# A test of all softmax row sums on the chip, with a second program behind a branch, and a newly written order of all work

## The chip, the core and the metric

The kernel runs on one core of one Trainium2 chip. A core has five engines, each with its own queue of instructions: TensorE (PE in the profile, its weight loads PEld), VectorE (DVE), ScalarE (ACT), GpSimd (POOL) and SyncE (SP, which here only issues transfers and waits). They meet only through semaphores. The metric is device microseconds of one execution; less is better. The profile is of one execution of the program on the chip, and it has a time of its own.

## The reference

For 2048 tokens `x` of width 512 the kernel computes a mix of two branches, `g * a + (1 - g) * b`, with one gate per token, `g = sigmoid(sum(x * gate_w))`.

Branch `a` is attention with 32 heads of width 16 over 4 segments of 512 tokens each, with a memory that is carried from segment to segment:

```
logits = einsum('bhqd,bhkd->bhqk', qs, ks) * scale + mask
p = softmax(logits, axis=-1)
a_dot = einsum('bhqk,bhkd->bhqd', p, vs)
num = einsum('bhld,bhde->bhle', phi(qs), M);  den = einsum('bhld,bhd->bhl', phi(qs), z) + 1e-6
o = g_head * num / den + (1 - g_head) * a_dot
M = M + einsum('bhld,bhle->bhde', phi(ks), vs);  z = z + sum(phi(ks))
```

`phi(t)` is `t + 1` above zero and `exp(t)` below; the mask is causal within a segment; `a` is `o @ wo`. Branch `b` is a gated feed-forward block: `(gelu(x @ w_gate) * (x @ w_up)) @ w_down`, 512 to 1792 to 512. Everything is given and returned in bf16. The reference's softmax subtracts the largest logit of each row before it takes the exponential.

## The kernel before, in words

The kernel takes the exponential of the scaled logits as they are, without a row maximum. The row sums come out of the same product as the weighted values: the tile of values, `vnat`, has a 17th column of ones for each head, so row 16 of each product is the sum of that row's exponentials. Both are turned by VectorE, the sum is inverted (`rc`, L650) and multiplied in (L651).

The work is cut into small tasks. A task names its engine, the instructions and the keys of what it reads and writes; `Emitter.plan` and `Emitter.finalize` derive from these keys every semaphore wait. In which order the tasks stand in each engine's queue is written out by hand, as one long string `ORDER` (L850 to L930): `Sched.schedule` walks through its words, and each word is a task's name, with the PSUM bank that it takes behind a colon, or `a` or `d` where the task may go to ScalarE or VectorE. No time is computed when the kernel is built; an engine runs its tasks strictly in this order and waits where one is not ready.

For each segment `s` and each tile there are these tasks:

- `K`, `Q`, `V`, `G`, `U`: products of four matmuls of 128x512 into one of four PSUM banks (`dense`, L446), each followed by an eviction `Kev`, `Qev`, `Vev`, `Gev` on ScalarE (L438) or VectorE (L439), or by the GELU (`gd`, `gelu`, ScalarE) or the product with it (`h`, VectorE, L689).
- `st`: a fill, logits of four heads at once into the one score tile `psX` of 128x2048 (L597); `exp`: the exponential of all of it on ScalarE (L603); `msk`: the causal mask of the diagonal blocks on GpSimd (L609). There are 72 fills. As `psX` exists once, a fill waits for the exponential of the fill before it.
- `pv`: 64 small matmuls that multiply the exponentials with the values (L640); `tp`: VectorE turns the two banks (L516); `pvp`: the inverse of the row sums and the scaling (L650, L651); `ot`: adds the memory's part (L657) and turns the result (L659) for `wo`.
- `nz`, `nd`, `mz`, `gate` on TensorE and `ndp`, `nzp`, `mzacc`, `phq`, `phk` on other engines: the memory and the gate.
- `out` (L702) and `wo` (L719): the two output products; `wev` scales the first on ScalarE (L707) or VectorE (L710), `oev` on VectorE adds the second (L723), and `dma` stores 128 rows of the output (L728), the last row tile in two halves, one issued by SP and one by ScalarE.

Weights and `x` are loaded in the first third (L329, L333). TensorE begins with some matmuls on constants (`wake`, L368), then turns the first part of `x` (`xtr0`, L774). At the end SP waits for each of the 17 output stores (L827), and the closing of the block (L806) gathers all engines.

The last words of `ORDER` before:

```
... pv3_3:31 tp3_d31:0 out3_2_2 tp3_d30:1 out3_1_4 out3_2_3
out3_2_4 wev3_1:a dma11_0 pvp3_31 out3_3_0:1 pvp3_30 ot3_3 out3_3_1 wo3_0_0:0 oev3_0_0 dma12_0 wo3_1_0:3 out3_3_2
out3_3_3 out3_3_4 oev3_1_0 wo3_2_1:0 wo3_2_0:3 wev3_2:a wo3_3_0:2 oev3_2_1 oev3_2_0 wo3_3_1:0 wev3_3:a dma13_0
oev3_3_0 dma14_1 dma15_0 oev3_3_1 dma15_1
```

Of the kernel before, what the change touches and what calls it, by code (L numbers as in the profile page):

```python
# [16 lines left out]
H = 32  # L17
# [6 lines left out]
ZMAX = 60.0  # L24
R_PT = 6
# [115 lines left out]


class Emitter:
# [75 lines left out]
    def emit(self, eng):  # L219
        e = self.engmap[eng]  # L220
        for spec in self.streams[eng]:
            for sem, val in spec.waits:
                e.wait_ge(sem, val)
            ins = spec.fn(e)
            if spec.dma_sem is not None:
                ins.then_inc(spec.dma_sem, 16)
            elif spec.inc:
                ins.then_inc(self.cnt[eng], 1)
# [7 lines left out]
def _build(es, nc, A_x, A_wq, A_wk, A_wv, A_wo, A_beta, B_w_gate, B_w_up, B_w_down, gate_w, out):  # L236
# [45 lines left out]
    rc = [sb(f"rc{i}", [P, 16], F32) for i in range(R_TT)]  # L282
# [14 lines left out]
    S = Sched({"bank": N_BANK, "X": 1, "tT": R_TT})  # L297
    I = Instr

    def task(name, ways, lat):  # L300
        return S.add(Task(name, ways, lat))

    def one(name, eng, est, instrs, lat=None):
        if lat is None:
            lat = {PE: L_PE, ACT: L_ACT, DVE: L_DVE, POOL: L_POOL, SP: 0.0}[eng]
        return S.add(Task(name, [(eng, est, instrs)], lat))

    def bk(s):
        return ("bank", s)


    def load(name, eng, fn, writes, issue=0.52, lat=2.5, size=0.0, wait=()):
        t = one("ld_" + name, eng, issue, [I(fn, wait, [*writes, ("ld", name)], sem("s_" + name))],
                lat=lat)
        t.size = size

    wgr = B_w_gate.rearrange("(kb p) n -> p kb n", p=P)
    wur = B_w_up.rearrange("(kb p) n -> p kb n", p=P)
    wdr = B_w_down.rearrange("(fb p) n -> p fb n", p=P)
    wsrc = lambda a: a.rearrange("(kb p) n -> p kb n", p=P)  # L320
    halves = (slice(0, 2), slice(2, 4))
    ball = omem[:, 1, 0:H]
    stage = (R_PT - 1,)

    def x_of(i, kb):
        return [("xT", i, kb, q) for q in range(4)]

    def ld_w(name, eng, dst, src, writes, size, wait=()):
        load(name, eng, lambda e: e.dma_start(dst, src), writes, size=size, wait=[("ld", w) for w in wait])  # L329

    def ld_xt(s, behind="wo30"):
        for kb in range(4):
            load(f"x{s}_{kb}", SP, lambda e, kb=kb: e.dma_start_transpose(  # L333
                xT[s % R_XT][:, kb, :], A_x[0, s * 512:(s + 1) * 512, kb * 128:(kb + 1) * 128]),
                x_of(s % R_XT, kb), issue=1.31, size=0.28, wait=[("ld", behind)])

    for q, (eng, n) in enumerate(((SP, 1), (ACT, 1), (SP, 2))):
        ld_w(f"x0_{q}", eng, pt[stage[0]][:, q:q + n, :],
             A_x[0, 128 * q:128 * (q + n), :].rearrange("(q p) d -> p q d", p=P), [("xs", q + j) for j in range(n)],
             0.125 * n)  # L340
    for h, eng in enumerate((ACT, SP)):
        ld_w(f"wk{h}", eng, wk[:, halves[h], :], wsrc(A_wk)[:, halves[h], :], [("wk", 2 * h), ("wk", 2 * h + 1)], 0.25)
    for h in range(2):
        ld_w(f"wq{h}", SP, wq[:, halves[h], :], wsrc(A_wq)[:, halves[h], :], [("wq", h)], 0.25)
    load("gw", SP, lambda e: e.dma_start(gatew[:, :], gate_w.rearrange("(kb p) -> p kb", p=P),
                                         allow_slow_non_contiguous=True), [("gatew",)], wait=[("ld", "x0_2")])
    ld_w("wv", SP, wv[:], wsrc(A_wv), [("wv",)], 0.5, ["x0_2"])
    ld_w("beta", SP, ball, A_beta.partition_broadcast(P), [("ball",)], 0.02, ["wk0"])
    ld_xt(1, "wv")
    ld_w("wg0", SP, wg[:, halves[0], :], wgr[:, halves[0], :], [("wg", 0)], 0.9, ["wq0"])  # L350
    ld_w("wg1", SP, wg[:, halves[1], :], wgr[:, halves[1], :], [("wg", 1)], 0.9, ["wv"])
    ld_w("wu0", SP, wu[:, halves[0], :], wur[:, halves[0], :], [("wu", 0)], 0.9, ["x1_3"])
    ld_w("wu1", SP, wu[:, halves[1], :], wur[:, halves[1], :], [("wu", 1)], 0.9, ["wg0"])
    ld_w("wd0", SP, wd[:, 0:HFT, :], wdr[:, 0:HFT, :], [("wd", 0)], 0.9, ["wg1"])
    ld_w("wd1", SP, wd[:, HFT:NFT, :], wdr[:, HFT:NFT, :], [("wd", 1)], 0.9, ["wu0"])

    wo32 = A_wo.rearrange("(x i) n -> x i n", i=32)
    for t in range(4):
        for i, (c0, c1, x) in enumerate(((0, t + 1, t), (t + 1, 4, 4 * (t + 1) + 3))):
            if c0 < c1:  # L360
                ld_w(f"wo{t}{i}", SP, wo[32 * c0:32 * c1, t, :], wo32[x:x + 3 * (c1 - c0 - 1) + 1:3], [("wo", t, i)],
                     0.03125 * (c1 - c0), ["wu1"])
    ld_xt(2)


    s0 = Slot("X")
    for i, cols in enumerate(([512] * 5 + [128] * 3, [128] * 1)):
        one(f"wake{i}", PE, 3.2, [I(lambda e, c=c: e.matmul(  # L368
            XALL[:, 0:c], nc.const_aps.tensor(1.0, [P, P], BF), nc.const_aps.tensor(1.0, [P, c], BF),
            start=True, stop=True), [], [("X", s0)]) for c in cols])  # L370
    cn = [
        I(lambda e: e.memset(maskA[:], 0.0), writes=[("maskA",)]),
    ]
    for g in range(4):
        cn.append(I(lambda e, g=g: e.memset(maskA[32 * g:32 * g + 16, :], 1.0), [("maskA",)], [("maskA",)]))
    cn.append(I(lambda e: e.tensor_scalar(maskB[:], maskA[:], -1.0, 1.0, ALU.mult, ALU.add),
                [("maskA",)], [("maskB",)]))
    one("masks", POOL, 1.0, cn)
    one("vones0", DVE, 1.22, [I(lambda e: e.memset(vnat[0][:, :, :, :, 16:17], 1.0),
                               writes=[("vnat", 0, m) for m in range(4)])])  # L380

    for i in range(2):
        cc = ctri[i][:, :]
        one(f"causal{i}", POOL, 0.3, [
            I(lambda e, cc=cc: e.memset(cc, 1.0), writes=[("ctri", i)]),
            I(lambda e, cc=cc, i=i: e.affine_select(out=cc, in_=cc, compare_op=ALU.is_ge, fill=0.0, base=64 * i,
                                                    pattern=[[1, 64]], channel_multiplier=-1),
              [("ctri", i)], [("ctri", i)])])
    causal = ctri[1]
    one("causal", DVE, 0.1, [I(lambda e: e.tensor_copy(causal[0:64, :], ctri[0][0:64, :]), [("ctri", 0), ("ctri", 1)],  # L390
                               [("causal",)])])
    one("ident", POOL, 0.6, [
        I(lambda e: e.memset(ident[:], 0.0), writes=[("ident",)]),
        I(lambda e: e.affine_select(out=ident[:], in_=ident[:], compare_op=ALU.not_equal, fill=1.0, base=0,
                                    pattern=[[-1, 128]], channel_multiplier=1), [("ident",)], [("ident",)]),
    ])
    cn = [
        I(lambda e: e.memset(bdmask[:], 1.0), writes=[("bdmask",)]),
    ]
    cn.append(I(lambda e: e.affine_select(out=bdmask[:], in_=bdmask[:], compare_op=ALU.is_ge, fill=0.0, base=0,  # L400
                                          pattern=[[-16, 8]], channel_multiplier=1), [("bdmask",)], [("bdmask",)]))
    cn.append(I(lambda e: e.affine_select(out=bdmask[:], in_=bdmask[:], compare_op=ALU.is_ge, fill=0.0, base=15,
                                          pattern=[[16, 8]], channel_multiplier=-1), [("bdmask",)], [("bdmask",)]))

    for c in range(4):
        cn.append(I(lambda e, c=c: e.tensor_copy(zmask[:, c, 2 * c:8], bdmask[:, 0:8 - 2 * c]), [("bdmask",)], [("zmask",)]))
        if c:
            cn.append(I(lambda e, c=c: e.tensor_copy(zmask[:, c, 0:2 * c], bdmask[:, 8 - 2 * c:8]), [("bdmask",)], [("zmask",)]))
    cn.append(I(lambda e: e.memset(mzacc[:], 0.0), writes=[("mzacc",)]))
    cn.append(I(lambda e: e.memset(vnat[1][:, :, :, :, 16:17], 1.0), writes=[("vnat", 1, m) for m in range(4)]))  # L410
    one("consts", POOL, 4.2, cn)


    def gate_products(h, sl):
        one(f"gate{h}", PE, 0.5, [I(lambda e, i=i, kb=kb, s=s: e.matmul(  # L415
            BK[sl.i][32 * i:32 * i + 1, 256 + 128 * (s % 2):384 + 128 * (s % 2)], gatew[:, kb:kb + 1],
            xT[s % R_XT][:, kb, :].rearrange("p (q j r) -> p j q r", j=4, r=32)[:, i],
# [88 lines left out]
    def slot_of(t, g):  # L506
        return (t - g) % 4

    def quad(c):
        return slice(32 * c, 32 * c + 32)  # L510
# [448 lines left out]
```

## Time and profile before

| what | value |
|---|---|
| median of 3 runs | 265.19 us (265.04 to 265.82) |
| the profiled execution's own time | 265.16 us |
| its span, first to last instruction | 263.4 us |
| time outside the span | 1.76 us |
| granted TensorE clock | 1.00 of full speed |
| PE busy | 259.6 us of the span |
| DVE, ACT, POOL busy | 200.3, 210.7, 96.4 us |

A page of the profile has numbered parts: 1 is the busy time of each engine, 2 the span in 40 slices of 6.6 us with the busy share in tenths, 3 the transfer queues, 4 the chain of work that ended last, 5 the costliest groups of instructions with what ended the idle time before them, 6 the issued transfers. Beside it the trace answers with the instructions in order of time (a timeline: start, duration, engine, line, operation, output and inputs), with the durations of one line's instructions, with who waited for whom, and with the busy time of each engine in a given stretch. Register, branch, semaphore and transfer-issuing instructions belong to an engine's sequencer (a "q" behind its name) and don't count as busy. The ends of matmuls are modelled, so that their durations overlap; from start to start a 128x512 matmul takes 0.216 us here.

### The profile page before, as it was taken

What the parts mean: (1) busy time and instruction counts of PE and PEld (TensorE: products, weight loads), DVE (VectorE), ACT (ScalarE), POOL (GpSimd) and SP (SyncE); (2) the same over time, 40 slices, a digit from 0 to 9 for tenths busy, and PEclk for the clock granted to TensorE, in tenths of its full rate; (3) what the DMA queues carried; (4) which work ended last, traced back from release to release, by engine and by line L of the source; (5) the groups of instructions that cost most, each with busy time, mean ns of one, the idle gap of its engine ahead of it and who ended that gap; (6) DMA issues with size and microseconds to landing.
All of it is one profiled execution on the core that took longest, in us unless ns stands there. A gap on an engine that the chain in (4) does not pass through costs nothing.

```text
span 263.4 us, 6630 instructions
## 1 busy us (share of the span) xinstructions
PE 259.6 (99%) x2829; PEld 113.4 (43%) x2829; DVE 200.3 (76%) x373; ACT 210.7 (80%) x174; POOL 96.4 (37%) x159
## 2 busy tenths in 40 slices
PE   8999999999999999999999999999999999999996
PEld 4633434444343443544434344444444443444443
DVE  1577767678896775988999998866779786865964
ACT  3589799998888978999888698759989968478612
POOL 6025233055536106144351844423635044152700
PEclk9999999999999999999999999999999999999999
DMA  7996188910045210000005200010002000010002
GB/s 229 281 184 169 37 109 194 257 56 2 0 55 99 70 40 0 2 4 20 2 0 85 59 2 2 20 33 0 2 4 74 2 2 0 2 60 2 20 2 80
DMA packets 24155, 14.92 MB, mean 57 GB/s; under 512 B 14526, under 2 KB 23102, under 8 KB 24126
## 3 DMA queue, kind: packets, MB, share of 16 engines
q1 hardware_dynamic: 23566, 14.04, 24.5%
q8 instruction: 22, 0.36, 0.6%
q10 hardware_dynamic: 560, 0.46, 0.5%
q14 instruction: 7, 0.06, 0.1%
HBM read 8.14 MB, written 2.10 MB: 39 GB/s over the span
## 4 chain that ended last, share of the span: by engine, by line
PE 97%; DMA 1%; DVE 0%; SPq 0%; issue 0%
PE psD L446 53%; PE psD L702 19%; PE psX L597 9%; PE psD L640 7%; PE psD L719 5%; DMA pt<-in_A_x_dram 1%; PE psD L468 1%; PE psD L474 1%; PE psD L565 1%; PE psD L415 0%; PE psX L541 0%; PE psD L531 0%; DVE ost L723 0%; PE psX L774 0%; SPq L329 0%
## 5 line engine op out<-in xcount | busy, mean ns | idle before, releaser
L603 ACT ACTIVATE pt<-psX 128x2048 bf16<-128x2048 f32 x72 | 135.1, 1876 | 31.7 <-PE psX L597 31.0
L609 POOL TENSOR_TENSOR pt<-pt,ctri 128x256 bf16<-128x256 bf16 x128 | 91.2, 720 | 152.0 <-ACT pt L603 147.6
L446 PE MATMUL psD<-xT,wu 128*128 128x512 bf16 x224 | 56.7, 380 | 0.0
L446 PE MATMUL psD<-xT,wg 128*128 128x512 bf16 x224 | 55.0, 380 | 0.0
L702 PE MATMUL psD<-wd,gb 128*128 128x512 bf16 x224 | 54.7, 380 | 0.0
L689 DVE TENSOR_TENSOR gb<-psD,gb 128x512 bf16<-128x512 f32 x56 | 37.3, 683 | 15.0 <-PE psD L446 14.7
L702 PEld LDWEIGHTS psD<-wd,gb 128*128 128x128 bf16 x224 | 20.4, 98 | 25.9 <-issue 3.3
L446 PEld LDWEIGHTS psD<-xT,wu 128*128 128x128 bf16 x224 | 20.2, 98 | 26.1 <-issue 3.4
L446 PEld LDWEIGHTS psD<-xT,wg 128*128 128x128 bf16 x224 | 20.3, 98 | 25.9 <-issue 3.0
L516 DVE STREAM_TRANSPOSE tT<-psD 128x512 f32<-128x512 f32 x35 | 24.1, 703 | 8.5 <-PE psD L640 8.0
L597 PE MATMUL psX<-qT,kD 32*128 32x192 bf16 (+7 forms) x512 | 28.5, 287 | 0.0
L597 PEld LDWEIGHTS psX<-qT,kD 32*128 32x128 bf16 x512 | 8.2, 92 | 24.9 <-ACT pt L603 18.9
L640 PE MATMUL psD<-pt,vnat 64*17 64x128 bf16 (+7 forms) x512 | 18.7, 283 | 0.0
L640 PE MATMUL psD<-pt,vsh 64*17 64x128 bf16 (+7 forms) x512 | 18.3, 283 | 0.0
L651 DVE SCALAR_TENSOR_TENSOR ob<-tT,gq,rc 128x256 bf16<-128x256 f32 x32 | 17.1, 534 | 1.1
L446 PE MATMUL psD<-wv,xT 128*128 128x512 bf16 x64 | 17.3, 380 | 0.0
L723 DVE SCALAR_TENSOR_TENSOR ost<-psD,gtok,wds 128x512 bf16<-128x512 f32 (+1 forms) x18 | 12.2, 686 | 6.2 <-PE psD L719 6.1
L446 PE MATMUL psD<-xT,wq 128*128 128x512 bf16 x64 | 16.6, 380 | 0.0
L719 PE MATMUL psD<-wo,oT 128*128 128x512 bf16 (+1 forms) x72 | 16.2, 356 | 0.0
L640 PEld LDWEIGHTS psD<-pt,vnat 64*17 64x17 bf16 x512 | 11.6, 86 | 8.7 <-POOL pt L609 4.0
L680 ACT ACTIVATE gb<-psD 128x512 bf16<-128x512 f32 x28 | 14.9, 606 | 0.3 <-PE psD L446 0.2
L439 DVE CAST gb<-psD 128x512 bf16<-128x512 f32 x18 | 11.9, 681 | 4.0 <-PE psD L446 4.0
(95 smaller groups left out, 253.9 us busy)
## 6 DMA issues: line engine op xcount, KB each, us to landing
out_dram<-ost SPq DMA_DIRECT2D x15, 128.0 KB, 1.8
wg<-in_B_w_gate_dram SPq DMA_DIRECT2D x2, 896.0 KB, 6.7
wu<-in_B_w_up_dram SPq DMA_DIRECT2D x2, 896.0 KB, 5.7
wd<-in_B_w_down_dram SPq DMA_DIRECT2D x2, 896.0 KB, 7.5
vsh<-vnat SPq DMA_DIRECT2D x16, 68.0 KB, 2.2
wq<-in_A_wq_dram SPq DMA_DIRECT2D x2, 256.0 KB, 5.1
wv<-in_A_wv_dram SPq DMA_DIRECT2D x1, 512.0 KB, 5.2
wk<-in_A_wk_dram ACTq DMA_DIRECT2D x1, 256.0 KB, 3.9
```

The source lines that it names most:

```text
L446: one(f"{name}{'abcd'[h // 2]}", PE, 2 * T_MM, [I(lambda e, i=i: e.matmul(BK[sl.i][:, :], lhs(i), rhs(i), start=(i == 0), stop=(i == n - 1 ...
L516: one(f"tp{name}", DVE, 0.605, [I(lambda e, ts=ts, bank=bank: e.transpose(tT[ts.i][:, :], bank()), [key], [("tT", ts)])])
L597: ins.append(I(lambda e, c=c, kb=kb, ncol=ncol, c0=c0, g=g: e.matmul(XALL[:, g * 512 + c0:g * 512 + c0 + ncol], kD[b][quad(g), c, kb, :], ...
L603: one(f"exp{s}_{name}", ACT, 2048 * 0.000833 + 0.05, [I(lambda e: e.activation(pt[slot][:, :, :], xin, ACTF.Exp, scale=ATT_SCALE), [("X", ...
L609: ins.append(I(lambda e, mv=mv: e.tensor_tensor(mv, mv, cm, ALU.mult), [("pt", slot), ("causal",)], [("pt", slot)]))
L640: ins.append(I(lambda e, kb=kb, slot=slot, c0=c0, n=n, g=g, c=c, r0=r0, sl=banks[j], va=va: e.matmul(BK[sl.i][32 * c:32 * c + 17, 64 * kb: ...
L651: I(lambda e, ts=ts, t=t, j=j, dst=dst: e.scalar_tensor_tensor(out=dst, in0=t_rows(ts, 16), scalar=gq[:, 2 * t + j:2 * t + j + 1], in1=rc_ ...
L680: one(f"gd{s}_{ft}", ACT, 0.485, [I(lambda e, gi=gi, f=f, sl=sl: e.activation(gb[gi][:, f, :], BK[sl.i][:, :], ACTF.Gelu_apprx_tanh), [bk( ...
L689: one(f"h{s}_{ft}", DVE, 0.605, [I(lambda e, sl=sl, gi=gi, f=f: e.tensor_tensor(gb[gi][:, f, :], BK[sl.i][:, :], gb[gi][:, f, :], ALU.mult ...
L702: mm.append(I(lambda e, fb=fb, gi=gi, f=f, q=q, sl=sl: e.matmul(BK[sl.i][:, :], gb[gi][:, f, q], wd[:, fb, :], start=(fb == 0), stop=(fb = ...
L719: one(f"wo{s}_{qt}_{ci}", PE, 4 * T_MM / len(parts), [I(lambda e, kb=kb, q=q, so=so, c=c: e.matmul(BK[so.i][:, c], oT[:, kb, q], wo[:, kb, ...
L723: lambda e, so=so, gt=gt, wi=wi, oi=oi, c=c: e.scalar_tensor_tensor(out=ost[oi][:, c], in0=BK[so.i][:, c], scalar=gtok[:, gt:gt + 1], in1= ...
```

## The change

Three things change.

**The test.** The inverted row sums no longer go to three rotating small tiles, but to `rcall`, one place for each of two segments, four tiles and two halves (128x128 numbers for a segment). After the four attention tiles of a segment, VectorE tests all of them (`chk0` to `chk3`): clamp to 1e-10 and 1e10, compare with the unclamped, take the minimum over the row. At the end `okrow` takes the minimum over the four segments, TensorE sums it over the 128 partitions (`oksum`, one matmul with one column), VectorE copies the sum to SBUF (`flag`), and each of the five engines loads it into a register (`reg_pe` and so on).

**The second program.** The build function is wrapped into `program(exact)` and called twice. Behind the first program each engine compares its register with 128.0 and, where it differs, runs the second program, the whole computation again with row maxima subtracted; where it is equal, it jumps over it. The second program doubles each fill's matmuls, and adds 512 products with two VectorE instructions each, three terms for each maximum, and 96 small transfers in each segment. SP's waits for the 17 stores stand behind the jump.

**The order.** `ORDER` is written anew for all tasks, with the new ones in it. 36 evictions change between ScalarE and VectorE; on balance six move to VectorE.

The core of the diff, without the re-indentation:

```diff
+RC_LO, RC_HI = 1e-10, 1e10
+GOOD = 0x43000000
...
-    rc = [sb(f"rc{i}", [P, 16], F32) for i in range(R_TT)]
+    rcall = sb("rcall", [P, 2, 4, 2, 16], F32)
+    okall = sb("okall", [P, NSEG], F32)
+    okrow = sb("okrow", [P, 1])
+    flag = sb("flag", [1, 1], F32)
...
+    def program(exact):
...
-                        qT[b][quad(g), c, 512 - ncol:512], start=True, stop=True, tile_position=(32 * g, 0)),
+                        qT[b][quad(g), c, 512 - ncol:512], start=True, stop=not exact, tile_position=(32 * g, 0)),
...
+                r, kr = rcall[:, b, t, j, :], ("rc", b, t, j)
                 one(f"pvp{s}_{t}{j}", DVE, 0.70, [
-                I(lambda e, ts=ts: e.reciprocal(rc[ts.i][:, :], tT[ts.i][:, 16:512:32]), [("tT", ts)], [("rc", ts)]),
+                    I(lambda e, ts=ts, r=r: e.reciprocal(r, tT[ts.i][:, 16:512:32]), [("tT", ts)], [kr]),
...
+        def test_rows(s):
+            r = rcall[:, s % 2].rearrange("p t j c -> p (t j c)")
+            kr = [("rc", s % 2, t, j) for t in range(4) for j in range(2)]
+            y = gt[:, 0:128]
+            one(f"chk{s}", DVE, 0.7, [
+                I(lambda e: e.tensor_scalar(y, r, RC_LO, RC_HI, ALU.max, ALU.min), kr, [("gt",)]),
+                I(lambda e: e.tensor_tensor(y, y, r, ALU.is_equal), [*kr, ("gt",)], [("gt",)]),
+                I(lambda e: e.tensor_reduce(okall[:, s:s + 1], y, mybir.AxisListType.X, ALU.min), [("gt",)], [("ok", s)])])
+            if s < NSEG - 1:
+                return
+            one("okrow", DVE, 0.1, [I(lambda e: e.tensor_reduce(okrow[:, :], okall[:, :], mybir.AxisListType.X, ALU.min),
+                                      [("ok", i) for i in range(NSEG)], [("okrow",)])])
+            sl = Slot()
+            one("oksum", PE, 0.1, [I(lambda e: e.matmul(BK[sl.i][:, 0:1], nc.const_aps.tensor(1.0, [P, P], BF), okrow[:, :],
+                                                        start=True, stop=True), [("okrow",)], [bk(sl)])])
+            one("flag", DVE, 0.1, [I(lambda e: e.tensor_copy(flag[:, :], BK[sl.i][0:1, 0:1]), [bk(sl)], [("flag",)])])
+
+            def fetch(e, eng):
+                regs[eng] = e.alloc_register(f"ok_{eng}")
+                return e.reg_load(regs[eng], flag.bitcast(mybir.dt.int32)[0:1, 0:1])
+
+            for eng in ENGINES:
+                one(f"reg_{eng}", eng, 0.1, [I(lambda e, eng=eng: fetch(e, eng), [("flag",)])])
...
+    def run(e, eng):
+        em.emit(eng, parts[0][eng])
+        with e.If_ne(regs[eng], GOOD):
+            em.emit(eng, parts[1][eng])
...
         @block.sync
         def _(e):
-            em.emit(SP)
+            em.emit(SP, parts[0][SP])
+            with e.If_ne(regs[SP], GOOD):
+                em.emit(SP, parts[1][SP])
+                for name in outs:
+                    e.wait_ge(sem(name), 32)
             for name in outs:
                 e.wait_ge(sem(name), 16)
...
 ORDER = """
...
+wev3_1:a tp3_d30:2 tp3_d31:1 out3_2_4 pvp3_30 pvp3_31 out3_3_0:1 out3_3_1 ot3_3 wo3_0_0:0 oev3_0_0 wo3_1_0:3 oev3_1_0
+out3_3_2 dma12_0 out3_3_3 chk3 wev3_2:a out3_3_4 okrow wo3_2_0:0 oev3_2_0 wo3_2_1:3 oev3_2_1 wo3_3_0:2 dma13_0
+wev3_3:a wo3_3_1:0 oev3_3_0 oev3_3_1 dma14_1 dma15_1 oksum:3 flag dma15_0 reg_pe reg_act reg_dve reg_pool reg_sp
```

## The prediction

> **What bounds the kernel now.** I read the page's head and queues first, then the busy time of each engine in three stretches, then the chain of work, and last the end of the run instruction by instruction.
>
> ```profile
> span 263.4 us, 6630 instructions
> PE 259.6 (99%) x2829; PEld 113.4 (43%) x2829; DVE 200.3 (76%) x373; ACT 210.7 (80%) x174; POOL 96.4 (37%) x159
> DVE  1577767678896775988999998866779786865964
> ...
> q8 instruction: 22, 0.36, 0.6%
> ...
> q14 instruction: 7, 0.06, 0.1%
> ...
> PE 97%; DMA 1%; DVE 0%; SPq 0%; issue 0%
> ```
>
> ```profile
> 4.86:260.82 255.96, 255.93 (x2812) 111.48 (x2812) 199.19 (x370) 209.16 (x173) 93.24 (x137) 1.00 0.25 54
> 260.82:263.40 2.58, 0.00 (x0) 0.00 (x0) 0.52 (x2) 0.00 (x0) 0.00 (x0) 1.00 0.33 102
> ```
>
> The columns of the second view are the stretch, its length, and the busy time of PE, PEld, DVE, ACT and POOL, then clock, transfer share and GB/s. TensorE has work in 255.93 of the 255.96 us from 4.86 to 260.82, at full clock. Its modelled ends could hide gaps, so I took the starts too: of 550 pairs of neighbouring 128x512 matmuls at L446 the mean distance is 217 ns and the usual one 216, and the distance before a fill is 316 on average with 309 to 312 as the usual one. Over the whole stretch I find some 0.4 us that a better order could still take out. The time is thus 4.9 us of start, 256 us of TensorE, and a tail of 2.6 us without TensorE, which is the stretch that the change reaches:
>
> ```profile
> 258.91 1.91 PE L719 MATMUL psD<-wo,oT 128*128 128x256 bf16 x16
> 259.11 0.69 ACT L707 ACTIVATE wds<-psD,omgt 128x512 f32<-128x512 f32 x1 [1.07 <-PE psD L702]
> 259.55 1.80 DVE L723 SCALAR_TENSOR_TENSOR ost<-psD,gtok,wds 128x256 bf16<-128x256 f32 x4 [1.41 <-PE psD L719]
> 261.38 0.36 ACTq L728 DMA_DIRECT2D out_dram<-ost  x1
> ```
>
> ```profile
> L806 PEldq DRAIN  x1: 775/775/775, 260.1 to 260.1; - x1
> ...
> L806 SPq COMPARE_BRANCH  x1: 41/41/41, 263.0 to 263.0; - x1
> L806 SPq DRAIN  x1: 13/13/13, 263.2 to 263.2; - x1
> ```
>
> ```profile
> L827 SPq EVENT_SEMAPHORE  x8: 28/28/28, 261.4 to 263.0; - x8
> ```
>
> The last VectorE instruction ends at 261.34, ScalarE issues the last store at 261.38, and it lands 1.6 us later (the page has 1.6 for both half stores). SP's eight waits lie between 261.36 and 262.96; those with nothing to wait for start 0.07 us apart. Then SP branches and drains, and the block closes 0.47 us after the last wait. TensorE is through at 260.87 and waits for the others.
>
> **The change, part by part.** The sum is made against the profiled execution's 265.16 us (span 263.4 and 1.76 around it), which is 0.03 below the median.
>
> *TensorE's work.* No matmul is taken out, one is added (`oksum`). Counting neighbours in the two order strings, 54 fills instead of 56 come right behind a product of the 128x512 kind and 15 instead of 14 behind a `pv`; at some 0.1 us for such a switch that is 0.1 to 0.2 us either way. All 72 fills stand in the same sequence, with the same 2.16 us of products between most of them. The start loads the same tiles in the same queue order, and its last wait is for the same part of `x`. I take 0, with −0.4 as the lower end.
>
> *VectorE's work.* `chk` is a 128x128 tensor_scalar (L537: 0.22 median), a tensor_tensor (L571, 128x136: 0.29) and a reduction (L762, a quarter of the size: 0.19; I take 0.28): 0.8 us, four times 3.2. Six evictions more are 5 by 0.69 (L439) and one by 0.75 (L710), 4.2; `okrow` and `flag` are small, 0.19 (L762) and 0.16 (the small copies at L742). So 7.7 us more, 208 of 263; ScalarE gets some 3.7 less. I hide it beside TensorE, and looked where the cover is thin. From `st1_2A` to `st2_2A`, around 107 to 165 us, where the slices show nines, the tasks add up to 58.9 us instead of 59.6 by the mean durations, so nothing is added there. From `st3_3A` to the end it is 23.3 instead of 16.6, against some 23 of TensorE. There the narrowest place is `wev3_0`, which moves to VectorE and must free the bank for `pv3_3`. Behind `pv3_2`'s result (VectorE starts at 241.62) VectorE has a turn 0.62, `pvp` 0.75, `chk2` 0.8, `h3_9` 0.62, `oev` 0.70, `ot` 1.3, a turn 0.62, two `pvp` 1.5, `ot` 1.3 and `wev3_0` 0.70 (distances of starts in the trace), 8.9: 250.5, seen by TensorE at 250.7. `pv3_3` began at 250.68 before, and with one pair of `U3_9` moved behind `pv3_2` is due at 251.1. It fits by 0.4. `chk3` and `okrow`, 1.0, fit in the 1.41 us idle ahead of the last stores' sums. Cost 0; if a cover fails, each slip is a few tenths, and I bound the whole at 1.5 (a fifth of the added work).
>
> *SP and GpSimd.* SP gets only `reg_sp`, behind the last issue; GpSimd's masks keep their work and sit with over 60% of the span idle. In front of the tail both cost 0.
>
> *The flag.* `oksum` stands behind the last `wo` and has its bank from `oev3_2_1`, so it runs while VectorE is still at the last `oev`: 0. `flag` then follows on VectorE: 261.34 + 0.16 = 261.50. Behind the flag's wait nothing but the register load, the branch and, on SP, the 17 waits is queued; the stores have been issued.
>
> *The register load.* No row shows one. It is a round trip of a sequencer to SBUF: below stands a register move on GpSimd (0.03), above the whole way of a store from issue to landing (1.6). I take half of the latter, 0.8, as one direction without the data's write. By the Trainium skill ("DMA: Bandwidth & Descriptors", latency and other measured facts) a tensor_load costs at least some 600 ns; no run here shows it, and by it the sum would be 0.2 lower.
>
> *The jump.* SP's branch at L806 shows 0.18 from its start to the next instruction. Behind it comes the question whether the target is at hand. The page shows instructions coming in all through the run: 22 blocks of 16 KB on q8 (2829 matmuls and as many weight loads at 64 bytes are just 0.36 MB, so this is TensorE) and 7 of 8 KB on q14. From the shares, 0.6% of 16 engines' span over 22 blocks is 1.15 us a block, and q14 about 0.6. By the diff the body jumped over holds about 3,900 matmuls with their weight loads on TensorE (490 KB), 1,800 instructions on VectorE (115 KB) and 460 transfers on SP (30 KB), so their targets lie several blocks on. Lower end: 0, a target already there. Upper end: the longest transfer record of such a block in the trace, 1.45, behind a transfer's fixed part, 1.2 (a store's 1.6 without some 0.4 of data), 2.65. As blocks come in order and the target is far, I take the fetch: 1.2 + 0.5 = 1.7 for SP, 1.2 + 1.15 = 2.35 for TensorE. The Trainium skill ("Runtime: NRT & Kernel Launch", instruction fetch mechanics) says that a taken branch whose target lies outside the current two pages stalls for its page, which speaks against this change; without that stall the sum would be 265.3, with it 267.0. The in-order blocks of the trace agree, no row shows a jump that misses.
>
> *The sum.* SP: 261.50 + 0.8 + 0.18 + 1.7 = 264.2; then eight or nine waits, all satisfied by now, 0.55: 264.75; then the close, 0.47: 265.2. TensorE: 261.50 + 0.8 + 0.18 + 2.35 = 264.85, and a drain and the close, 0.4: 265.2. Both give a span of 265.2, 1.8 more than before, and 265.16 + 1.8 = 267.0 us.
>
> **The rivals.**
>
> *A, the tail hides, not slower.* The last store lands at 262.96 whatever the flag does. If load and fetch take x together, SP is through its waits at 261.50 + x + 0.18 + 0.55; the end moves by under 0.8 us (0.3%, about what a measurement can tell here) as long as x is below 1.5. It needs a target at hand or a quick fetch. For it speaks only that the bounds begin at 0.03; against it the blocks in order. Time 265.2 to 265.9, at its middle 265.6.
>
> *B, load and fetch at their upper ends.* Five engines load one word and fetch at once. With 1.6 and 2.65, SP ends at 261.50 + 4.43 + 0.55 + 0.47 = 266.95, so 3.5 more: 268.7. For it: the page's shortest landing of any transfer is 1.6.
>
> *C, VectorE becomes late in the body.* If `wev3_0` or a `chk` slips behind TensorE's need and a fifth of the added 7.7 us comes out, 1.5 on top of the sum: 268.5. It decides when the segment-3 sum above exceeds its 0.4 of room. Against it: the counts.
>
> *D, the second program runs.* Then the time would more than double, over 530. The sums of at most 512 exponentials of small logits lie far inside the bounds.
>
> **How the numbers follow.** The sum's own case, 266.1 to 268.0, gets 0.46, A 0.17, B 0.20, C 0.14, D under 0.01, and 0.02 are left for an order that gains its 0.4 with a hidden tail and more. So slower 0.80, same 0.17, faster 0.03. Predicted 267.0. The range reaches into A down to 265.7 and through B and C up to 269.2.
>
> **What would show it.** Right: PE busy without gaps until about 260.8; `flag` close to 261.5; a register load and a branch on each engine behind it; some microsecond of nothing, with one instruction block on q8 and q14 in it; SP's waits all 0.07 apart, without a wait for a landing. Wrong: gaps of PE before `pv3_3` or a fill with VectorE as releaser (C); SP still waiting for the last store (A); loads and gaps of 2 us and more (B). The term most open is load plus fetch; if the prediction fails, I expect it there.

## The result, and the profile after

| what | before | after |
|---|---|---|
| median | 265.41 us (265.04 to 265.82) | 269.0 us (268.7 to 270.44) |
| ratio, with its 95% interval | | 1.0146 (1.0106 to 1.0186) |
| the profiled execution | 265.16 us | 268.7 us |
| its span | 263.4 us | 266.9 us |

The changed kernel is 1.5% slower: 3.6 us, where the prediction had 1.8. In the profiled executions, too, it is 3.5 us, and all of that lies inside the span. First the head of the page, the queues of instruction blocks and the chain of work:

```profile
span 266.9 us, 6643 instructions
...
PE 259.2 (97%) x2830; PEld 113.0 (42%) x2830; DVE 207.3 (78%) x393; ACT 208.2 (78%) x168; POOL 96.7 (36%) x159
...
DVE  1855853789889478989988999777988787778771
...
q8 instruction: 24, 0.39, 0.6%
...
q14 instruction: 15, 0.12, 0.2%
...
PE 96%; DMA 1%; DVE 0%; SPq 0%; issue 0%
```

VectorE has 7 us more work, as the change says, and TensorE as much as before. The two instruction queues, q8 (TensorE's) and q14 (the other four engines'), have fetched two and eight blocks more. The busy time by stretches (stretch, length, then PE, PEld, DVE, ACT, POOL, clock, transfer share, GB/s) says where the 3.5 us are:

```profile
4.86:260.62 255.76, 255.61 (x2813) 111.26 (x2813) 206.44 (x391) 206.32 (x166) 93.52 (x137) 1.00 0.24 54
260.62:266.90 6.28, 0.01 (x2) 0.00 (x0) 0.58 (x3) 0.00 (x0) 0.00 (x0) 0.74 0.19 57
```

Up to 260.6 us TensorE is busy in 255.61 of 255.76 us; the body has not become longer. The tail without TensorE was 2.6 us and is now 6.3. Its beginning, in order of time (start, duration, engine, line, operation, output and inputs, idle time with its releaser):

```profile
257.86 0.22 DVE L716 TENSOR_SCALAR gt<-rcall 128x128 f32<-128x128 f32 x1
258.11 0.29 DVE L717 TENSOR_TENSOR gt<-gt,rcall 128x128 f32<-128x128 f32 x1
258.43 0.29 DVE L718 TENSOR_REDUCE okall<-gt 128x1 f32<-128x128 f32 x1
258.75 0.16 DVE L721 TENSOR_REDUCE okrow<-okall 128x1 bf16<-128x4 f32 x1
259.35 1.79 DVE L846 SCALAR_TENSOR_TENSOR ost<-psD,gtok,wds 128x256 bf16<-128x256 f32 x4 [0.44 <-PE psD L842]
260.46 0.17 PE L724 MATMUL psD<-okrow,const-bfloat16-1.0 128*128 128x1 bf16 x1
261.06 0.13 DVE L726 COPY flag<-psD 1x1 f32<-1x1 f32 x1
```

The last test and `okrow` stand in the idle time ahead of the last sums (VectorE still waits 0.44 us for TensorE behind them), and the flag is there at 261.20. Then the sequencers (durations in ns as least, median, most; then first and last start; TensorE's stands there as PEldq). The register load:

```profile
L730 SPq TENSOR_LOAD <-flag x1: 585/585/585, 261.2 to 261.2; - x1
...
L730 PEldq TENSOR_LOAD <-flag x1: 625/625/625, 261.2 to 261.2; - x1
```

The branch behind it:

```profile
L943 POOLq COMPARE_BRANCH  x1: 45/45/45, 261.9 to 261.9; - x1
...
L943 PEldq COMPARE_BRANCH  x1: 3629/3629/3629, 261.9 to 261.9; - x1
```

```profile
L967 SPq COMPARE_BRANCH  x1: 58/58/58, 261.9 to 261.9; - x1
```

What stands behind the jump, SP's waits for the stores and the drains of the closing block:

```profile
L972 SPq EVENT_SEMAPHORE  x8: 27/28/28, 266.0 to 266.4; - x8
```

```profile
L947 PEldq DRAIN  x1: 73/73/73, 265.6 to 265.6; - x1
...
L947 POOLq DRAIN  x1: 124/124/124, 266.1 to 266.1; - x1
L947 SPq COMPARE_BRANCH  x1: 43/43/43, 266.5 to 266.5; - x1
```

And the instruction blocks that came in behind 255 us (queue, packets, MB, share of the stretch):

```profile
q14 instruction: 8, 0.07, 1.9%
...
q8 instruction: 2, 0.03, 1.1%
```

All five engines branch at 261.86 to 262.09 us and none shows another instruction before 265.6. TensorE's branch is itself recorded as 3.63 us long; the others' as 0.05 to 0.07, with nothing behind them for 4.0 to 4.2 us (SP: branch 261.86, first wait 265.97). SP's waits then follow each other at once; the last store has long landed. The trace's transfer records place the fetch in this hole: four blocks of 8 KB begin at 262.82 to 263.02 and have ended by 263.40, one of 16 KB runs from 262.94 to 264.15. So it takes about 1.0 us from the branch to the first byte, 0.4 to 0.5 for a block (1.2 for TensorE's), and then SP still does nothing for 2.6 us, TensorE for 1.5.

### The profile page after: what moved, and what is told of

Read it like the earlier page. It is cut to its first block, busy times and chain, and to the rows that moved or that the text cites. A ratio compares the mean times of both kernels' runs of the same rounds, so it can differ in the third digit from the quotient of the medians.

```text
span 266.9 us, 6643 instructions
## 1 busy us (share of the span) xinstructions
PE 259.2 (97%) x2830; PEld 113.0 (42%) x2830; DVE 207.3 (78%) x393; ACT 208.2 (78%) x168; POOL 96.7 (36%) x159
## 4 chain that ended last, share of the span: by engine, by line
PE 96%; DMA 1%; DVE 0%; SPq 0%; issue 0%
PE psD L482 53%; PE psD L825 19%; PE psX L633 9%; PE psD L686 7%; PE psD L842 5%; DMA pt<-in_A_x_dram 1%; PE psD L504 1%; PE psD L510 1%; PE psD L601 1%; PE psD L451 0%; PE psX L577 0%; PE psD L567 0%; DVE ost L846 0%; PE psX L897 0%; SPq L352 0%
## 5 line engine op out<-in xcount | busy, mean ns | idle before, releaser
L698 DVE SCALAR_TENSOR_TENSOR ob<-tT,gq,rcall 128x256 bf16<-128x256 f32 x32 | 17.9, 559 | 1.1
L482 PE MATMUL psD<-xT,wq 128*128 128x512 bf16 x64 | 17.4, 380 | 0.0
## 6 DMA issues: line engine op xcount, KB each, us to landing
out_dram<-ost SPq DMA_DIRECT2D x15, 128.0 KB, 1.7
```

The source lines that it names most:

```text
L482: one(f"{name}{'abcd'[h // 2]}", PE, 2 * T_MM, [I(lambda e, i=i: e.matmul(BK[sl.i][:, :], lhs(i), rhs(i), start=(i == 0), stop=(i == n - 1 ...
L698: I(lambda e, ts=ts, t=t, j=j, dst=dst, r=r: e.scalar_tensor_tensor(out=dst, in0=t_rows(ts, 16), scalar=gq[:, 2 * t + j:2 * t + j + 1], in ...
```

## Experiments

The theory is that all of the 3.5 us is the jump to a place that is not at hand. Its rivals are the body (order, test) and the tail (load, branch, waits) for themselves. "Gap" below is the time from the start of an engine's branch to the start of its next instruction.

### The order alone

The kernel before, with the new `ORDER` in which the new tasks' words are left out:

```diff
 ORDER = """
...
-oev3_3_0 dma14_1 dma15_0 oev3_3_1 dma15_1
+oev3_3_0 oev3_3_1 dma14_1 dma15_1 dma15_0
```

> The kernel before with the new order of work alone: no test, no flag, no loads, no jumps. Both theories use it as the zero of the other runs. The last matmul began 0.2 us earlier in the changed kernel, so F expects a span of 263.2 and a time of 264.9 to 265.1 us, 0.1 to 0.3 below the kernel before. If the order is what costs (O), 265.6 or more.

Measured: 265.57 us, ratio 1.0003 (0.9993 to 1.0013). The order, with its 36 changed evictions, costs and brings nothing that can be measured. The 0.1 to 0.3 us less that was expected did not come either: it rested on the last matmul of `wo`, which starts 0.2 us earlier in the changed kernel's trace (260.35 against 260.55), but in this run's it starts at 260.95.

### The test without the jump

The changed kernel without the branches and the second program; with nobody to use them, the register loads fall away too:

```diff
 def run(e, eng):
     em.emit(eng, parts[0][eng])
-    with e.If_ne(regs[eng], GOOD):
-        em.emit(eng, parts[1][eng])
```

> The changed kernel without the jumps and the second program; the test and the flag stay, and the register loads fall away with the jumps that read them. The output is the same as long as the test passes. Theory F (the block with the jump's target has to be fetched, some 4 us, and this is the whole loss): the tail is again the landing of the last store, which is issued at 261.2 and lands 1.6 later, so the span is 263.2 to 263.4 and the time about 265.1 us, 0 to 0.3 below the kernel before. Theory O (the new order or the test's work costs time in the body): the span stays above 264, the time above 265.9.

Measured: 265.68 us, ratio 1.0021 (0.9993 to 1.005), between the 265.1 of the one theory and the 265.9 of the other; the profiled execution has a span of 263.5. SP leaves its waits as it did before:

```profile
L945 SPq COMPARE_BRANCH  x1: 41/41/41, 263.1 to 263.1; - x1
```

The four tests, the matmul and the flag cost at most half a percent, and no cost at all lies within the interval. What is left for the jump, the load and what they leave standing is thus about 269.0 − 265.7, 3.3 us of the 3.6.

### The jump with a near target

The changed kernel with its loads and branches, but only the first instructions of the second program left for each engine to jump over, so that the guard does not work:

```diff
     with e.If_ne(regs[eng], GOOD):
-        em.emit(eng, parts[1][eng])
+        first = parts[1][eng].start
+        em.emit(eng, slice(first, min(first + 2, parts[1][eng].stop)))
```

and the same with 100 and with 300 in the place of 2. 300 instructions of TensorE are 600 with their weight loads; GpSimd has only 175 in its whole second program.

> The changed kernel with its loads and jumps, but the body that is jumped over is cut to the first two tasks' instructions on each engine, so that the target lies next to the jump (the part jumped over is no longer a working second program). F: the target is at hand, SP is at its waits at about 262.1 and then waits for the last store until 262.8; span 263.2 to 263.5, time 265.0 to 265.3 us. Theory J (a taken conditional jump on five engines costs some 4 us wherever it goes): span 266.9, time 268.7 us as the changed kernel.

> The changed kernel with the body cut to the first 100 tasks' instructions on each engine (6.4 KB; 12.8 KB on TensorE): the jump is longer than in body_2, but the target lies in the block after the present one at most, and the rows of the instruction queues show blocks of 8 and 16 KB arriving one ahead. F: no gap, SP at its waits 0.2 us behind the branch, span 263.2 to 264. If only the block that is running counts: one or more engines show the gap of 4 us, span near 266.9.

> The same with up to 300 tasks' instructions (19 KB on SP and VectorE, 38 KB on TensorE, all of the second program on ScalarE and GpSimd, which have about 170). The targets lie beyond the next block of SP and VectorE. F: gap of 4 us on SP and VectorE, span 266.5 to 267.3, time 268.3 to 269.1 us; whether TensorE has one tells whether it holds more than two of its blocks.

With 2: 265.57 us, ratio 1.0019 (1.0 to 1.0038). TensorE's branch and SP's waits:

```profile
L943 PEldq COMPARE_BRANCH  x1: 215/215/215, 261.9 to 261.9; - x1
```

```profile
L972 SPq EVENT_SEMAPHORE  x8: 28/28/28, 262.1 to 262.8; - x8
```

Here the test, the flag, the load and five branches together cost at most 0.4%: SP's gap is 0.2 us, and it then waits for the last store as before. With 100 (one execution, 265.28 us, span 263.5) no engine has a gap above 0.6 us:

```profile
L943 PEldq COMPARE_BRANCH  x1: 350/350/350, 262.1 to 262.1; - x1
```

```profile
L972 SPq EVENT_SEMAPHORE  x8: 28/28/28, 262.6 to 263.0; - x8
```

With 300 (one execution, 269.09 us, span 267.3) the whole hole is back, on all five:

```profile
L943 PEldq COMPARE_BRANCH  x1: 3569/3569/3569, 262.3 to 262.3; - x1
```

```profile
L972 SPq EVENT_SEMAPHORE  x8: 28/28/28, 266.4 to 266.8; - x8
```

The cost is a step somewhere between the two: nothing at 100 instructions, all of it at 300, and no more for the whole second program (SP's gap 4.09 us here, 4.11 there; TensorE's 3.63 here, and 3.69 for its thousands of matmuls). At 64 bytes, TensorE's 200 instructions are 12.8 KB and its 600 are 38 KB, in blocks of 16 KB; for the others it is 6.4 KB against 11 to 19 KB, in blocks of 8 KB, and the separate semaphore waits between the instructions, which are not counted here, add to that. This is what the Trainium skill ("Runtime: NRT & Kernel Launch", instruction fetch mechanics) states of a taken branch whose target lies outside the two current pages. The runs agree in that the near targets cost nothing and the far ones a standstill; just where the limit lies they do not show.

### One engine alone

Load, branch and second program on one engine only, the others have none, so that the guard does not work: for SP, for GpSimd, and for TensorE.

```diff
 def run(e, eng):
     em.emit(eng, parts[0][eng])
-    with e.If_ne(regs[eng], GOOD):
-        em.emit(eng, parts[1][eng])
+    if eng == POOL:
+        with e.If_ne(regs[eng], GOOD):
+            em.emit(eng, parts[1][eng])
```

> The changed kernel with the load, the jump and the second program's part on SP alone; the other four engines have neither, so this is no working guard. Theory F (each engine waits for its own block): SP's gap from the branch to its first wait is again 4.1 us, span 266.5 to 267.2, time 268.3 to 269.0 us. Theory C (five engines that fetch at once make each other slow): alone the gap is near the predicted 1.9 us, span 264.5 to 265.0, time 266.3 to 266.8 us.

> GpSimd alone has the load, the branch and its second program; the other four engines have neither, so the second program could not run as a whole and the guard does not work here. In pool_mid GpSimd was the only engine whose target was missing, and still stood still for 3.7 us, where SP alone needed 2.6; but in pool_mid the other four fetched their following blocks in the same microsecond. Theory 1, blocks that are fetched at the same time, whoever waits for them, lengthen the standstill: here nothing else is fetched and the gap of GpSimd is that of SP alone, 2.4 to 2.8 us, GpSimd's drain at about 264.2 to 264.6, span 264.4 to 265.2, time 266.2 to 267. Theory 2, it is GpSimd's own and longer than SP's: gap 3.5 to 4.2, span 265.6 to 266.6, time 267.4 to 268.4.

> TensorE alone has the load, the branch and its second program; the guard does not work here. Its block is 16 KB and took 1.2 us in the changed kernel where the others' 8 KB took 0.4. Theory 1, the crowd costs over a microsecond: the branch that lasted 3.63 us lasts 2.2 to 3.1, TensorE's drain at 264.2 to 265.0, span 264.5 to 265.3. Theory 2, TensorE's standstill is its own block's: 3.5 to 3.8, span 265.6 to 266.2.

One execution each: SP 267.78 us (span 265.7), GpSimd 266.88 (264.9), TensorE 268.18 (266.2). SP's branch, and what ends the gap: SP's first wait, GpSimd's drain, and for TensorE the length of the branch:

```profile
L965 SPq COMPARE_BRANCH  x1: 58/58/58, 262.2 to 262.2; - x1
```

```profile
L970 SPq EVENT_SEMAPHORE  x8: 28/28/28, 264.8 to 265.3; - x8
```

```profile
L948 POOLq DRAIN  x1: 123/123/123, 264.5 to 264.5; - x1
```

```profile
L944 PEldq COMPARE_BRANCH  x1: 3469/3469/3469, 262.3 to 262.3; - x1
```

| engine | gap alone | gap with all five | alone: branch to fetch, block, block's end to next instruction |
|---|---|---|---|
| SP | 2.61 us | 4.11 us | 0.93, 0.53, 1.15 |
| GpSimd | 2.74 us | 4.2 us | 0.97, 0.57, 1.20 |
| TensorE | 3.53 us | 3.7 us | 0.98, 1.07, 1.49 |

For SP and GpSimd some 1.5 us of the gap is company: the fetch begins as soon as alone, the block takes as long, and the wait behind the block grows from 1.2 to 2.6 us. For SP neither theory held (4.1 or some 1.9 expected, 2.61 found). For GpSimd the theory of company held (2.4 to 2.8 expected, 2.74 found). For TensorE it failed: its standstill is almost all its own. TensorE alone takes 268.18 us against the 265.23 of an execution of the kernel before beside it, 2.95 of the 3.6; some 0.2 of that is a body that ended later in it (the last matmul of `wo` starts at 260.77, in the trace before at 260.55).

### A hint ahead of the branch

An instruction that stands ahead of a branch can name it and its target (BRANCH_PREFETCH_HINT in the trace, where it lasts 0.04 to 0.06 us). The whole guard with both programs is kept; each engine gets one such hint, so many instructions before the end of its first program:

```diff
+EARLY = {PE: 41, ACT: 33, DVE: 116, POOL: 17, SP: 58}
...
-        for spec in self.streams[eng][part]:
+        specs = self.streams[eng][part]
+        for n, spec in enumerate(specs):
+            if early and n == len(specs) - early:
+                self.loc[eng] = e.mark_branch_hint_location()
...
+        bass.BassInstruction(br[0]).branch_hint(em.loc[eng])
```

This is `hint_early`. `hint` differs in the counts alone (PE 41, ACT 4, DVE 12, POOL 2, SP 5), `pool_first` and `pool_mid` only in that GpSimd's is 130 and 50 instead of 17.

> The changed kernel with the whole second program, and on each engine one instruction some microseconds ahead of the jump that announces the jump as likely taken (on TensorE before its last 41 matmuls, on the others 2 to 12 tasks ahead), so that the target's block can be fetched in time. F: the gap of 4 us behind the branch shrinks to some 0.2 us where the announcement lies over 4 us ahead; span 263.3 to 264.5, time 265.1 to 266.3 us. J, or an announcement that does not bring the block: span 266.9, time 268.7 us.

> As the run hint, with the announcement on the four engines that did not use it moved ahead of the last moment at which each fetched a block in sequence (ScalarE to about 193 us, VectorE 186, GpSimd 222, SP 27; TensorE as it was, where the announcement worked). If an announcement is taken up only when an engine goes on to a next block, these four now fetch the target in time: span 263.3 to 264, time 265.1 to 265.9 us. If they ignore it: span 266.5 to 268, as in the run hint.

> The whole guard, both programs. Only the place of GpSimd's hint differs from hint_early: there it stood 17 of GpSimd's instructions before the end (221.7 us) and GpSimd alone still stood still for 3.9 us; here it stands 130 before the end, about 13 to 18 us into the span. Theory 1, a hint is taken up when its engine goes on to its next block, and GpSimd last did so before 221 us (the blocks that the trace shows at 36 to 65 us): GpSimd goes on within 0.6 us of its branch as the other four did, the last store's landing at about 262.5 to 263 sets the end again, span 263.2 to 263.9, time 265.1 to 265.8, ratio to the kernel before 0.999 to 1.003. Theory 2, GpSimd does not use a hint, or only one given shortly before the branch: it misses again, gap 3.7 to 4.2, span 266 to 266.9, time 268 to 269.2.

> As pool_first, with GpSimd's hint 50 instructions before the end (about 110 to 150 us). If GpSimd goes on to a next block for the last time at 36 to 65 us, the hint comes too late and GpSimd alone stands still for 3.7 to 4.2 us: span 266 to 266.9, time 268 to 269.2. If it goes on at 231 us and the hint of hint_early, ten us ahead of that, was only too close to it, this hint works: span 263.2 to 263.9, time 265.1 to 265.8. Together with pool_first the two say which it is; if both miss, GpSimd does not take hints.

| kernel | hints at, in us of the span: PE, ACT, DVE, POOL, SP | engines with a gap of 3.7 us or more | time | ratio, 95% |
|---|---|---|---|---|
| `hint` | 252.5, 253.8, 255.8, 249.7, 245.7 | ACT, DVE, POOL, SP | 270.39 us | 1.0185 (1.0138 to 1.0232) |
| `hint_early` | 251.5, 191.2, 184.3, 221.7, 26.1 | POOL | 269.2 us | 1.0156 (1.0069 to 1.0243) |
| `pool_mid` | 252.2, 191.9, 185.0, 162.4, 26.5 | POOL | 268.48 us | 1.0122 (1.0086 to 1.0157) |
| `pool_first` | 252.4, 192.1, 185.1, 20.1, 26.5 | none | 265.77 us | 1.002 (0.999 to 1.0049) |

By the theory both `hint` and `hint_early` were to end near the kernel before, and neither did. In `hint` only TensorE used its hint: its branch fell from 3.63 to 0.41 us, and the trace has its extra 16 KB block at 256.2 us, but SP went on only after 4.26 us:

```profile
L949 PEldq COMPARE_BRANCH  x1: 405/405/405, 262.8 to 262.8; - x1
```

```profile
L989 SPq EVENT_SEMAPHORE  x8: 27/28/28, 267.0 to 267.5; - x8
```

That `hint` comes out 1.4 us above the changed kernel without hints is not shown to be a cost of the hints: the two intervals overlap, and in its trace the body ended 0.9 us later (the last matmul of `wo` starts at 261.25 instead of 260.35).

In `hint_early` SP was through its waits at 262.9 us and GpSimd alone held the end:

```profile
L989 SPq EVENT_SEMAPHORE  x8: 28/28/28, 262.4 to 262.9; - x8
```

```profile
L963 POOLq DRAIN  x1: 116/116/116, 265.7 to 265.7; - x1
```

In `pool_first` no engine stands still:

```profile
L963 POOLq DRAIN  x1: 112/112/112, 263.2 to 263.2; - x1
...
L963 SPq COMPARE_BRANCH  x1: 53/53/53, 263.8 to 263.8; - x1
```

This is the whole guard, at a time that cannot be told from the kernel before. It is not faster than it: the body is full, and nothing of the guard was to be gained. The profiled execution's span, 264.2, is 0.8 above before's 263.4; 0.6 of that is a body that ended later in it (the last matmul of `wo` starts at 261.16 instead of 260.55), and the tail from there is 3.0 us instead of 2.9.

Which hint works fits the theory that it is taken up when the engine goes on to its next block of instructions. TensorE does so every 12 us on average, the others rarely (seven blocks of 8 KB in the whole span ahead of the branch), and each of the other four missed a late hint and used an early one; GpSimd's last chance lies between 20.1 and 162.4 us. A lead that is merely too short is no rival: GpSimd's hint failed 100 us ahead of its branch, TensorE's worked 10 us ahead. The transfer records fit too: in `hint_early`, `pool_mid` and `pool_first` the block that the changed kernel and `hint` fetch at 231 to 232 us is missing and one comes at 202 to 203 us in its place, soon after the early hints of VectorE and ScalarE. Which of the seven blocks belongs to which engine the trace does not say, so this rule is argued from the four kernels, not shown block by block.

## Why the prediction was wrong in size

The direction and the place were right: the body did not change, and the end went to load, branch and fetch, where the prediction expected to fail if it did. The mechanism, engines that stand still until the block with the target has been fetched, was right as well, but incomplete. One term of the sum was mis-sized by it, the fetch: 1.7 us for SP and 2.35 for TensorE, where branch and fetch together took 4.11 and 3.7.

| term of the sum | predicted | measured |
|---|---|---|
| body (order, 7.7 us of VectorE work) | 0 | 0 (order alone 1.0003) |
| one `chk` | 0.8 us | 0.22 + 0.29 + 0.29 = 0.80 us |
| flag done | 261.50 | 261.20 |
| register load | 0.8 us | 0.66 us on SP from flag to branch, 0.59 of it the load |
| SP: branch and fetch | 0.18 + 1.7 us | 4.11 us |
| TensorE: branch and fetch | 0.18 + 2.35 us | 3.7 us |
| SP's waits | 0.55 us | 0.50 us |
| close | 0.47 us | 0.44 us |

Along SP the terms are off by −0.3 (flag), −0.14 (load), +2.23 (branch and fetch) and −0.08 (waits, close), together +1.7, which takes the forecast span of 265.2 to the 266.9 found.

**What was wrong in the fetch.** The prediction built it as a transfer: a store's fixed part of 1.2 us and the block's data. The transfer is indeed no longer than that: 1.0 us to its start and 0.4 to 0.5 of data. Two things were left out. The engine does not go on when the block is in: alone it takes another 1.15 us (SP) to 1.5 (TensorE). And five engines at once stretch that, to 2.6 us on SP, though the blocks come no later. What fills this time, alone or in company, stays open. The upper bound, 2.65 us, was made of transfer rows too and so was no bound: a price without a row had been bounded by rows of another kind, which can't hold what comes after the transfer.

**The other steps.** The flag came 0.3 us earlier: the last matmul of `wo` starts 0.2 us sooner in this execution (260.35 instead of 260.55), and the flag's copy is recorded as beginning 0.08 us before the last sum's end. VectorE's added work is 7.0 us of busy time instead of 7.7, ScalarE lost 2.5 instead of 3.7; all of it is hidden, and `chk3` with `okrow` fitted into the idle time as reckoned. Of the 6.7 us that the prediction put behind `st3_3A`, 3.4 are there (VectorE is busy for 15.91 us from there to the end before and for 19.32 after). `wev3_0` was in time with more room than reckoned: it ends at 249.51 us instead of 250.5, and TensorE has 25.50 us of work in the 25.50 from 235 to 260.5. For the load, the floor of some 600 ns that the Trainium skill ("DMA: Bandwidth & Descriptors", latency and other measured facts) gives for a tensor_load was nearer than the 0.8 taken from the store; ScalarE's load of 0.48 lies below it, and there the measurement decides.

**The rivals.** A, a hidden tail, fell with SP's waits 0.07 us apart behind the gap, none of them for a landing; but it is just what happens where the target is at hand, as the jump over two instructions, the jump over a hundred and `pool_first` show, at 265.3 to 265.8 us. B came out at its time, 268.7, for the profiled execution, but by luck: the load was 0.6, not 1.6, and SP's branch and fetch 4.1, not 2.83. C fell: TensorE has no gap in the body. D did not happen.

## What to carry to other kernels

A branch over a large body is not paid by the branch but by the instructions behind it: here some 3.5 us of standing still for a test that itself cost nothing that could be told. If such a guard is wanted, keep what it jumps over short (100 instructions cost nothing here, 300 all of it), or give the target ahead of time, and early: by the rule argued above, so early that each engine still goes on to another block after the hint. And when a price has no row in the profile, a bound from rows of another kind is only a guess; measure the jump by itself, on one engine and on all.

## What the runs showed of the hardware

- From a branch to a target that is not at hand to the next instruction it takes 2.6 to 2.7 us on SP and GpSimd alone, 3.5 on TensorE alone, and 3.7 to 4.2 us when all five branch. Of that only 0.4 to 1.2 us is the block's transfer.
- Company counts even if the others do not stand still: in `pool_mid` GpSimd was the only engine without its target and needed 3.7 us instead of 2.7, while the other four fetched their following blocks in the same stretch, from 263.5 to 264.7 us. What lengthens the wait behind the transfer was not found.
- A jump to a target at hand takes 0.2 to 0.3 us to the next instruction where it is close by (two instructions skipped; VectorE 0.6), and 0.4 to 0.6 us where it lies further on (100 skipped) or has been fetched by a hint.
- TensorE's instructions come in blocks of 16 KB and the other engines' in blocks of 8 KB: where one engine alone jumps, the hole holds one block of 8 KB on q14 for SP and for GpSimd, and one of 16 KB on q8 for TensorE.
- A hint named BRANCH_PREFETCH_HINT in the trace takes the standstill away where it is used: TensorE's branch fell from 3.63 to 0.41 us, and with all five used the kernel took 265.77 us instead of 269.0.
